# Values with the probabilities held fixed in the first eleven heads, and a branch sum in four column groups

## The chip, the core and the metric

The kernel runs on one core of a Trainium2 chip. The metric is device time in microseconds. The kernel before takes 192.63 us, the median of 8 runs (192.5 to 192.9). The core has five engines with queues of their own: PE (matrix multiply), DVE (vector), ACT (activation functions), POOL and SP; here SP issues nearly all transfers. [...]

## What is computed

Two branches on the same two rows `x` (batch 2, one position, 448 wide), and the residual:

```python
xn = layernorm(x)
# A: attention of one new position, 16 heads on 8 key/value heads, W = 4096 last positions
q = xn @ wq                                    # 448 -> 16 heads x 256
scores = q . k[last 4096] * 256 ** -0.5
o = softmax(scores) . v[last 4096]
a = o.reshape(2, 4096) @ wo                    # 4096 -> 448
# B: dense with a mish activation
h = xn @ w1 + b1                               # 448 -> 1792
b = (h * tanh(softplus(h))) @ w2               # 1792 -> 448
out = x + a + b
```

The caches hold 2 MB of K and 2 MB of V for each of the 16 pairs of key/value head and batch row. With the weights that is 77.7 MB to read.

## The kernel before

**Heads.** The program calls a pair (key/value head, batch row) a head; there are `NK` = 16, numbered 0 to 15, and each serves `rep` = 2 query heads. Key/value head `kvh` has heads 2 kvh and 2 kvh + 1. A head's 4096 positions lie as `T` = 32 tiles of 128 positions over the partitions, and are worked on in two halves of 16 tiles.

**A head's stages.**
- `load_k`, `load_v` (L327, L335): SP issues one 2 MB transfer each, K into one of 4 buffers, V into one of 5. The last V is cut into a half and two quarters. `load_wo` (L343) brings the slice of `wo` for a key/value head, the last one in two parts.
- `turn` (L352): DVE transposes half of K in 32x32 blocks.
- `scores` (L362): PE, 8 matmuls of 512 columns with a spread-out copy of q (`qdiag`, built by POOL in `build_q`, L241) as stationary operand; then ACT takes the exponential of 128x512 scores and their row sums.
- `turn_p` (L387): DVE transposes the probabilities. After the second half it forms `sums` by two small operations with the selector `hsel`; a small fp32 matmul, `den`, adds over the partitions, and DVE takes the reciprocal `rec`.
- `values` (L407): for each of 32 tiles and 2 column sets PE loads 128x128 of V as weights and streams the 2 columns of probabilities past it, 64 pairs of load and matmul, into a PSUM buffer (`ps_o`, 2 of them). DVE then scales by `rec` into `oT`, in bf16.
- `mix` (L433), once for each key/value head: the branch sum. PE multiplies `oT` (two stationary columns, one for each batch row) with the slice of `wo`, 8 matmuls of 224 columns.

**The branch sum's place.** The two output rows are summed in PSUM over the whole kernel, in `psA[0]` and `psA[1]`, 2x224 each, one bank each. `x` itself goes in first (2 matmuls, L209), then branch B (`dense_out`, L309, 28 matmuls, in loop turn 1), then the eight `mix`. At the end DVE copies one half to `res`, ACT the other, and one store writes the two rows.

**Order.** Every engine runs its instructions in the order in which the program writes them (`issue_in_order`, L17). Loop turn i (L457) issues the loads of K of head i+2 and V of head i, then the turns and scores of head i, with the probabilities turned one half later, then `build_q`, then `values` of head i-2 (`KA` = 2), and after an odd head its `mix`. Two further turns, 16 and 17, hold only the values of the last heads:

```python
        if i >= KA:
            values(i - KA)
            kvh, b = heads[i - KA]
            if b == Bsz - 1:
                mix(kvh)
```

So on PE a head's 64 value pairs stand behind the scores of the head two later, and DVE's scaling stands behind the turns of that later head.

Of the kernel before, what the change touches and what calls it, by code (L numbers as in the profile page):

```python
# [9 lines left out]
ALU = mybir.AluOpType  # L10
AXIS = mybir.AxisListType
BF16 = mybir.dt.bfloat16
FP32 = mybir.dt.float32
PSUM = bass.MemoryType.PSUM
# [20 lines left out]
def kernel(  # L35
# [13 lines left out]
    nc = tc.nc  # L49
    P = 128  # L50
    Q = 32
    NQ = P // Q

    Bsz, Sq, D = A_x.shape
    _, Hkv, Sk, Dh = A_k_cache.shape
    HqDh = A_wq.shape[1]
    Hq = HqDh // Dh
    rep = Hq // Hkv
# [3 lines left out]
    T = W // P  # L62
    NH = 2
    TH = T // NH
# [6 lines left out]
    ND = Dh // P  # L71
    NB = Dh // (2 * Q)
    NE = 2
    assert Sq == 1 and D * NX == NS * P and NS % 2 == 1 and HF % P == 0 and Hq % NX == 0
    assert TH * Q <= 512 and NB * NE * Q == Dh and ND == 2
    scale = float(Dh) ** -0.5
# [3 lines left out]
    ident = lead.tile([P, P], BF16)  # L80
    hsel = lead.tile([P, Q], FP32)
# [4 lines left out]
    consts = ctx.enter_context(tc.tile_pool(name="consts", bufs=1))  # L86
    p_pool = ctx.enter_context(tc.tile_pool(name="pp", bufs=3))
    small = ctx.enter_context(tc.tile_pool(name="small", bufs=3))
    ps_sc = ctx.enter_context(tc.tile_pool(name="ps_sc", bufs=2, space=PSUM))
    ps_o = ctx.enter_context(tc.tile_pool(name="ps_o", bufs=2, space=PSUM))  # L90
    ps_den = ctx.enter_context(tc.tile_pool(name="ps_den", bufs=1, space=PSUM))
    ps_a = ctx.enter_context(tc.tile_pool(name="ps_a", bufs=1, space=PSUM))
    ps_m = ctx.enter_context(tc.tile_pool(name="ps_m", bufs=1, space=PSUM))


    x_bf = consts.tile([Bsz, D], BF16)
# [14 lines left out]
    for lo, hi in ((0, SC), (SC, NS)):  # L111
        w = v_tile((hi - lo) * HW).rearrange("p (s n) -> p s n", n=HW)
# [2 lines left out]


    make_identity(nc, ident[:])
    eps_t = consts.tile([Bsz, 1], FP32)
    nc.vector.memset(eps_t[:], 1e-5)

# [7 lines left out]
        out=rstd[:], in_=mv[:, 1:2], func=ACT.Sqrt, bias=eps_t[:], scale=1.0  # L128
# [5 lines left out]
    for r in range(2):  # L134
        n = (NS + 1 - r) // 2
        nc.vector.tensor_scalar(  # L136
            out=xn_bf[:, r : NS : 2, :, :],
            in0=bass.AP(
                x_all.tensor,
                x_all.offset,  # L140
                [list(x_all.ap[0]), [1, n], [NS, P // 2], [(NS + r) // 2, 2]],
            ),
# [7 lines left out]
    for b4 in range(NB):  # L150
        rows = slice(b4 * Q, (b4 + 1) * Q)
        for j in range(NQ):
            nc.vector.tensor_copy(
                out=spread[rows, b4, j * Q : (j + 1) * Q], in_=ident[rows, rows]
            )
    hsel = hsel[:, 0:rep]
    nc.vector.tensor_copy(out=hsel, in_=ident[:, 0:rep])
    for j in range(1, NQ):
        nc.vector.tensor_tensor(
            out=hsel, in0=hsel, in1=ident[:, j * Q : j * Q + rep], op=ALU.add  # L160
        )
    ones_f = consts.tile([P, P], FP32)
    nc.gpsimd.memset(ones_f[:], 1.0)
# [2 lines left out]
    for i in range(NW):  # L166
        t = consts.tile([P, NB * NE, P], BF16, name=f"qdiag{i}")
# [5 lines left out]
    for s in range(NS):  # L173
# [7 lines left out]
        out=odd[:],  # L181
# [16 lines left out]
    nc.vector.memset(ones[:], 1.0)  # L198


    NO = 2
    DO = D // NO
    psA = [ps_a.tile([Bsz, DO], FP32, name=f"psA{n}") for n in range(NO)]

    def add(n, lhsT, rhs, **flags):
        nc.tensor.matmul(psA[n][:, :], lhsT=lhsT, rhs=rhs, skip_group_check=True, **flags)  # L206

    for n in range(NO):
        add(n, ident[0:Bsz, 0:Bsz], x_bf[:, n * DO : (n + 1) * DO], start=True, stop=False)  # L209


    qrep = consts.tile([P, NB, HH, NE, NX, Bsz], BF16)
# [28 lines left out]
    def build_q(i):  # L241
        kvh, b = heads[i]
        x, h0 = divmod(kvh * rep, HH)
        t = qdiag[i % NW]
        tv = t[:].rearrange("p (n e) c -> p n e c", e=NE)
        for j in range(NQ):
            rows = slice(j * Q, (j + 1) * Q)
            for e in range(NE):
                nc.gpsimd.tensor_copy(  # L249
                    out=tv[rows, :, e, j * Q : j * Q + rep],  # L250
                    in_=qrep[rows, :, h0 : h0 + rep, e, x, b],
                )

# [55 lines left out]
    def dense_out():  # L309
        w2_sb = dense.pop("w2")  # L310
        for x in range(NX):
            for c in range(NF):
                for n in range(NO):
                    add(
                        n,
                        act_bf[:, c, x, :],
                        w2_sb[:, x, c, n * DO : (n + 1) * DO],
                        start=False,
                        stop=False,
                    )  # L320


    NSTEP = len(heads) * NH
# [1 line left out]
    state = {}  # L325
# [26 lines left out]
    def turn(s):  # L352
        kt = kt_pool.tile([P, TH * Dh], BF16, tag="kt", name="kt")
        i, half = divmod(s, NH)
        k = k_t[i] if half < NH - 1 else k_t.pop(i)
        nc.vector.transpose(  # L356
            out=kt[:].bitcast(FP32),
            in_=k[:, half * TH * Dh : (half + 1) * TH * Dh].bitcast(FP32),
        )
        kt_t[s] = kt  # L360
# [26 lines left out]
    def turn_p(s):  # L387
        pT = p_pool.tile([P, TH * Q], BF16, tag="pT", name="pT", bufs=7)
        nc.vector.transpose(out=pT[:], in_=p_t.pop(s)[:])  # L389
        pT_t[s] = pT  # L390
        i, half = divmod(s, NH)
        if half != NH - 1:
            return
        rs = state.pop(("rs", i))
        sums = small.tile([P, rep], FP32, tag="sums", name="sums")
        nc.vector.tensor_scalar(
            out=sums[:], in0=hsel, scalar1=rs[:, 0:1], scalar2=None, op0=ALU.mult
        )
        nc.vector.scalar_tensor_tensor(  # L399
            out=sums[:], in0=hsel, scalar=rs[:, 1:2], in1=sums[:], op0=ALU.mult, op1=ALU.add  # L400
        )
        den = ps_den.tile([P, rep], FP32, tag="den", name="den")
        nc.tensor.matmul(den[:], lhsT=ones_f[:], rhs=sums[:], start=True, stop=True)  # L403
        state["rec", i] = small.tile([P, rep], FP32, tag="rec", name="rec", bufs=4)
        nc.vector.reciprocal(out=state["rec", i][:], in_=den[:])  # L405

    def values(i):  # L407
        kvh, b = heads[i]
        po = ps_o.tile([P, ND, rep], FP32, tag="o", name="o")
        vv = v_t.pop(i).rearrange("p t (m c) -> p t c m", c=ND)  # L410
        for t in range(T):
            half, th = divmod(t, TH)
            pTv = pT_t[i * NH + half][:].rearrange("p (t c) -> p t c", t=TH)
            for c in range(ND):
                nc.tensor.matmul(  # L415
                    po[:, c, :],
                    lhsT=vv[:, t, c, :],
                    rhs=pTv[:, th, 0:rep],
                    start=(t == 0 and c == 0),
                    stop=(t == T - 1),  # L420
                    skip_group_check=True,
                )
        if b == 0:
            state["oT"] = small.tile([P, ND, rep, Bsz], BF16, tag="oT", name="oT")
        oT = state["oT"]
        nc.vector.tensor_tensor(  # L426
            out=oT[:, :, :, b],
            in0=po[:],
            in1=state.pop(("rec", i))[:].unsqueeze(1).to_broadcast([P, ND, rep]),
            op=ALU.mult,  # L430
        )

    def mix(kvh):  # L433
        oT = state["oT"]
        w = wo_t.pop(kvh)
        for h in range(rep):
            for n in range(NO):
                for c in range(ND):
                    add(
                        n,  # L440
                        oT[:, c, h, :],
                        w[:, h, c * D + n * DO : c * D + (n + 1) * DO],
                        start=False,
                        stop=(kvh == Hkv - 1 and h == rep - 1 and c == ND - 1),
                    )

    NK = len(heads)
    KA = 2
# [5 lines left out]
    build_q(0)  # L454
    build_q(1)
    turn(0)
    for i in range(NK + KA):  # L457
        if i + 2 < NK:
            load_k(i + 2)
        if i < NK:  # L460
            load_v(i, (0, T) if i < NK - 1 else (0, T // 2, 3 * T // 4, T))
            kvh, b = heads[i]
            if b == Bsz - 1:
                load_wo(kvh, parts=1 if i < NK - 1 else 2)
            for half in range(NH):
                s = i * NH + half
                if s + 1 < NSTEP:
                    turn(s + 1)
                scores(s)
                if s >= 1:  # L470
                    turn_p(s - 1)
            if i + 2 < NK:
                build_q(i + 2)
        if i == NK:
            turn_p(NSTEP - 1)
        if i == 0:
            dense_in()
        if i == 1:
            dense_out()
        if i >= KA:  # L480
            values(i - KA)
            kvh, b = heads[i - KA]
            if b == Bsz - 1:
                mix(kvh)

    res = consts.tile([Bsz, D], BF16)
    nc.vector.tensor_copy(out=res[:, 0:DO], in_=psA[0][:, :])
    nc.scalar.copy(out=res[:, DO:D], in_=psA[1][:, :])  # L488
    nc.sync.dma_start(out=out.flatten_outer_dims(), in_=res[:])
    issue_in_order(tc)  # L490

# [29 lines left out]
```

The softmax here doesn't subtract the row's maximum and nothing guards it: scores larger than these inputs give would overflow.

## Time and profile before

| what | value |
|---|---|
| median of 8 runs | 192.63 us |
| the profiled execution | 192.62 us |
| its span (first to last instruction) | 190.7 us |
| mean granted clock of PE | 0.797 |
| busy: PE, its weight loads, DVE, ACT, POOL | 72%, 41%, 57%, 13%, 13% |
| PE loads and matmuls | 1592 each |
| data read | 77.67 MB, 407 GB/s over the span |

"Busy" is the time in which an engine runs at least one instruction, as a share of the span. A row of the page's groups reads: source line, engine, operation, output<-input, shape, count | busy time, mean duration in ns | idle time just before, and what ended it. The chain of work that ended last is followed back from the last instruction, each step to what released it. The row of slices cuts the span in 40 parts of 4.8 us and gives the busy share in tenths; for `PEclk` the clock that the throttle granted, 9 being 90% or more of full speed. Instruction counts of the built programs, and the arrival marks of a transfer's sixteen shares, are named as such.

### The profile page before, as it was taken

Reading aid. Unit: us, or ns where it says so; the run is one execution under the profiler, and the core shown is the slowest. Engines: PE = TensorE matmul, PEld = TensorE weight load, DVE = VectorE, ACT = ScalarE, POOL = GpSimd, SP = SyncE. Lnnn points to the kernel's source line nnn. Section 1 sums busy time; section 2 is a strip of 40 time slices with the busy share of each in tenths; the row PEclk is TensorE's granted clock in tenths of the full one; section 3 lists DMA queues with packets and bytes.
Section 4 is the critical chain, followed back from the end, with each engine's and each line's share of the span. In section 5 each row is a group of like instructions: output and inputs, shape, how many; then the busy total and the mean of one; then the engine's idle time right before and its main releaser. Section 6 shows DMA issues by size and latency. Waiting matters only on the chain.

```text
span 190.7 us, 3752 instructions
## 1 busy us (share of the span) xinstructions
PE 136.8 (72%) x1592; PEld 77.5 (41%) x1592; DVE 108.0 (57%) x169; ACT 25.4 (13%) x69; POOL 25.0 (13%) x139
## 2 busy tenths in 40 slices
PE   0242994699876959596759688696959493894984
PEld 0151373246552614344244435361535233362672
DVE  4706406895959390939366573939093754839301
ACT  5000110111210211011111111021102011021100
POOL 8005220010220201102020202020111100000000
PEclk9999995569996975888586957696678889589955
DMA  6999999999999999999999999999999999999970
GB/s 213 423 440 419 428 438 426 426 428 434 429 431 419 433 419 426 433 436 415 444 426 423 426 436 417 436 436 416 433 429 426 421 431 433 436 419 430 404 288 8
DMA packets 7818, 77.90 MB, mean 408 GB/s; under 512 B 757, under 2 KB 2809, under 8 KB 3322
## 3 DMA queue, kind: packets, MB, share of 16 engines
q1 hardware_dynamic: 7796, 77.66, 96.3%
q8 instruction: 12, 0.20, 0.4%
q14 instruction: 4, 0.03, 0.0%
q10 hardware_dynamic: 6, 0.01, 0.0%
HBM read 77.67 MB, written 0.00 MB: 407 GB/s over the span
## 4 chain that ended last, share of the span: by engine, by line
DMA 81%; DVE 8%; PE 8%; SPq 1%; issue 0%; ACT 0%
DMA k<-in_A_k_cache_dram 67%; DMA v<-in_A_v_cache_dram 13%; DVE kt L356 6%; PE sc L368 4%; PE psA L206 2%; DVE pT L389 1%; PE o L415 1%; SPq L113 0%; PE den L403 0%; SPq L260 0%; SPq L265 0%; SPq L330 0%; DVE oT L426 0%; DVE den_sb L305 0%; ACT res L488 0%
## 5 line engine op out<-in xcount | busy, mean ns | idle before, releaser
L356 DVE STREAM_TRANSPOSE kt<-k 128x2048 f32<-128x2048 f32 x32 | 73.5, 2299 | 44.4 <-DMA k<-in_A_k_cache_dram 44.4
L368 PE MATMUL sc<-kt,qdiag 128*128 128x512 bf16 x256 | 83.6, 484 | 15.7 <-DVE kt L356 12.2
L368 PEld LDWEIGHTS <-qdiag 128*128 128x128 bf16 x256 | 28.7, 121 | 56.4 <-issue 39.9
L378 ACT ACTIVATE p<-sc 128x512 bf16<-128x512 f32 x32 | 19.1, 598 | 144.8 <-PE sc L368 140.9
L249 POOL COPY qdiag<-qrep 32x8 bf16<-32x8 bf16 x128 | 21.0, 186 | 123.1 <-PE sc L368 108.3
L415 PEld LDWEIGHTS <-v 128*128 128x128 bf16 x1024 | 28.5, 98 | 5.7 <-issue 2.2
L415 PE MATMUL o<-pT,v 128*128 128x2 bf16 x1024 | 28.5, 163 | 0.9 <-DMA v<-in_A_v_cache_dram 0.8
L206 PE MATMUL psA<-wo,oT 128*2 128x224 bf16 x64 | 12.5, 370 | 14.5 <-DVE oT L426 14.5
L389 DVE STREAM_TRANSPOSE pT<-p 128x512 bf16<-128x512 bf16 x32 | 21.5, 671 | 0.0
L206 PEld LDWEIGHTS <-oT 128*2 128x2 bf16 x64 | 6.5, 111 | 17.8 <-DVE oT L426 15.2
L403 PEld LDWEIGHTS den<-sums,ones_f 128*128 128x128 f32 x32 | 6.5, 233 | 17.0 <-DVE sums L399 15.7
L403 PE MATMUL den<-sums,ones_f 128*128 128x2 f32 x32 | 6.5, 272 | 9.3 <-DVE sums L399 9.3
L405 DVE RECIPROCAL rec<-den 128x2 f32<-128x2 f32 x16 | 2.7, 170 | 16.0 <-PE den L403 16.0
L220 PE MATMUL qT_ps<-xs,v 128*128 128x4 bf16 x112 | 3.3, 166 | 5.5 <-DMA v<-in_A_wq_dram 3.0
L426 DVE TENSOR_TENSOR oT<-o,rec 128x4 bf16<-128x4 f32 x16 | 2.2, 136 | 7.4 <-PE o L415 7.4
L378 ACT ACTIVATION_READ_ACCUMULATOR p<-sc 128x1 f32 x32 | 6.2, 194 | 0.0
L220 PEld LDWEIGHTS <-v 128*128 128x128 bf16 x112 | 3.2, 104 | 6.0 <-DMA v<-in_A_wq_dram 6.0
L174 PE MATMUL xnT_ps<-ident,xn_bf 2*128 2x2 bf16 x7 | 0.5, 166 | 5.2 <-DVE xn_bf L136 5.2
L229 DVE CAST qT<-qT_ps 128x64 bf16<-128x64 f32 x1 | 0.2, 225 | 6.4 <-PE qT_ps L220 6.4
L399 DVE SCALAR_TENSOR_TENSOR sums<-hsel,rs,sums 128x2 f32<-128x2 f32 x16 | 3.5, 221 | 0.6
L275 PE MATMUL hT_ps<-xs,v 128*128 128x4 bf16 x49 | 3.7, 195 | 0.0
L275 PEld LDWEIGHTS <-v 128*128 128x128 bf16 x49 | 3.2, 151 | 0.3
(43 smaller groups left out, 28.3 us busy)
## 6 DMA issues: line engine op xcount, KB each, us to landing
k<-in_A_k_cache_dram SPq DMA_DIRECT2D x16, 2048.0 KB, 32.0
v<-in_A_v_cache_dram SPq DMA_DIRECT2D x15, 2048.0 KB, 35.0
v<-in_B_w_dram SPq DMA_DIRECT2D x2, 1568.0 KB, 21.0
wo<-in_A_wo_dram SPq DMA_DIRECT2D x7, 448.0 KB, 32.0
v<-in_A_wq_dram SPq DMA_DIRECT2D x1, 2048.0 KB
v<-in_A_wq_dram SPq DMA_DIRECT2D x1, 1536.0 KB, 10.7
v<-in_A_v_cache_dram SPq DMA_DIRECT2D x1, 1024.0 KB, 29.1
v<-in_A_v_cache_dram SPq DMA_DIRECT2D x2, 512.0 KB, 27.5
```

Of the source, the lines that this page charges most:

```text
L206: nc.tensor.matmul(psA[n][:, :], lhsT=lhsT, rhs=rhs, skip_group_check=True, **flags)
L220: nc.tensor.matmul(qT_ps[:, hh, e, :], lhsT=wq_v[s][:, hh, e, :], rhs=xs[:, s, :, :].rearrange("p x b -> p (x b)"), start=(s == 0), stop=( ...
L249: nc.gpsimd.tensor_copy(out=tv[rows, :, e, j * Q : j * Q + rep], in_=qrep[rows, :, h0 : h0 + rep, e, x, b],)
L275: nc.tensor.matmul(hT_ps[:, c, :, :].rearrange("p x b -> p (x b)"), lhsT=w1_v[:, s, c, :], rhs=xs[:, s, :, :].rearrange("p x b -> p (x b)" ...
L356: nc.vector.transpose(out=kt[:].bitcast(FP32), in_=k[:, half * TH * Dh : (half + 1) * TH * Dh].bitcast(FP32),)
L368: nc.tensor.matmul(psc[:], lhsT=qdiag[i % NW][:, n * NE + e, :], rhs=ktv[:, n, e, :, :], start=(n == 0 and e == 0), stop=(n == NB - 1 and ...
L378: nc.scalar.activation(out=p_sb[:], in_=psc[:].rearrange("p t c -> p (t c)"), func=ACT.Exp, scale=scale, accum_out=state["rs", i][:, s % N ...
L389: nc.vector.transpose(out=pT[:], in_=p_t.pop(s)[:])
L399: nc.vector.scalar_tensor_tensor(out=sums[:], in0=hsel, scalar=rs[:, 1:2], in1=sums[:], op0=ALU.mult, op1=ALU.add)
L403: nc.tensor.matmul(den[:], lhsT=ones_f[:], rhs=sums[:], start=True, stop=True)
L405: nc.vector.reciprocal(out=state["rec", i][:], in_=den[:])
L415: nc.tensor.matmul(po[:, c, :], lhsT=vv[:, t, c, :], rhs=pTv[:, th, 0:rep], start=(t == 0 and c == 0), stop=(t == T - 1), skip_group_check ...
```

## The change

Five things change:

1. **Values of heads 0 to 10** (`NFIX` = 5 heads stay as they were). The probabilities become the stationary operand: 4 columns, which are 2 tiles x 2 query heads. V streams past them, 2 tiles x 256 = 512 columns a matmul, 16 matmuls a head. Only the blocks in which a tile meets its own probabilities are used. ACT copies the 4x512 result to SBUF (`o_sb`).
2. **`finish`**, one head later, after the next head's first scores: four fp32 transposes on PE bring that result to 128 partitions in a PSUM buffer `q`; DVE copies one block and adds the other, then scales as before (`scale_o`).
3. **Heads 11 to 15** keep the 64 pairs (`values_fixed`), with the one buffer `q` as target. `mix` moves along: `close(i)` runs in the next loop turn for heads up to 13, for heads 14 and 15 right after their values. `mix(6)` thereby comes behind the last `den`.
4. **The branch sum** has four parts of 112 columns instead of two of 224. Each sits at its own PE column group (`tile_position=(0, 32 n)`) and its own 32 PSUM partitions, two parts to a bank. Each call of `add` issues four pairs. Four copies, two on DVE and two on ACT, bring the parts to the two rows of `res`; one store.
5. **Small parts.** The two query heads' columns lie 16 apart (`HS`) instead of side by side, in `hsel`, `build_q` and the probabilities. `den` shares a PSUM bank with earlier tiles (`ps_m`). DVE makes an fp32 identity at the start.

```diff
-    for n in range(NO):
-        add(n, ident[0:Bsz, 0:Bsz], x_bf[:, n * DO : (n + 1) * DO], start=True, stop=False)
+    NO = NQ
+    DO = D // NO
+    psA = [ps_a.tile([P, DO], FP32, name=f"psA{u}") for u in range(2)]
+
+    def part(n):
+        return psA[n // 2][n * Q : n * Q + Bsz, :]
+
+    def add(lhsT, w, start=False, stop=False):
+        for n in range(NO):
+            nc.tensor.matmul(
+                part(n),
+                lhsT=lhsT,
+                rhs=w[:, n * DO : (n + 1) * DO],
+                start=start,
+                stop=stop,
+                tile_position=(0, n * Q),
+                skip_group_check=True,
+            )
+
+    add(ident[0:Bsz, 0:Bsz], x_bf[:, :], start=True)
...
-                    out=tv[rows, :, e, j * Q : j * Q + rep],
+                    out=tv[rows, :, e, j * Q : (j + 1) * Q : HS],
...
     def values(i):
+        po = ps_o.tile([NR, NP * Dh], FP32, tag="o", name="o")
+        v = v_t.pop(i)
+        for u in range(T // NP):
+            half, uh = divmod(u, TH // NP)
+            nc.tensor.matmul(
+                po[:],
+                lhsT=pT_t[i * NH + half][:, uh * NP * Q : (uh + 1) * NP * Q : HS],
+                rhs=v[:, u * NP : (u + 1) * NP, :].rearrange("p t d -> p (t d)"),
+                start=(u == 0),
+                stop=(u == T // NP - 1),
+            )
+        o_sb = small.tile([NR, NP * Dh], FP32, tag="o_sb", name="o_sb", bufs=1)
+        nc.scalar.copy(out=o_sb[:], in_=po[:])
+        state["o", i] = o_sb
...
+    def finish(i):
+        ov = state.pop(("o", i))[:].rearrange("r (u m c) -> r u c m", u=NP, c=ND)
+        pq = ps_q.tile([P, NP * ND * NR], FP32, tag="q", name="q")
+        pqv = pq[:].rearrange("p (u c r) -> p u c r", u=NP, c=ND)
+        for u in range(NP):
+            for c in range(ND):
+                nc.tensor.transpose(pqv[:, u, c, :], ov[:, u, c, :], ident_f[0:NR, 0:NR])
+        o = small.tile([P, ND, rep], FP32, tag="osum", name="osum")
+        nc.vector.tensor_copy(out=o[:], in_=pqv[:, 0, :, 0:rep])
+        for u in range(1, NP):
+            nc.vector.tensor_tensor(
+                out=o[:], in0=o[:], in1=pqv[:, u, :, u * rep : (u + 1) * rep], op=ALU.add
+            )
+        scale_o(i, o[:])
...
+    NFIX = 5
+
+    def close(i):
+        if i < NK - NFIX:
+            finish(i)
+        kvh, b = heads[i]
+        if b == Bsz - 1:
+            mix(kvh)
+
     for i in range(NK + KA):
...
+                if half == 0 and i > KA:
+                    close(i - KA - 1)
...
         if i == NK:
             turn_p(NSTEP - 1)
+            close(i - KA - 1)
...
         if i >= KA:
-            values(i - KA)
-            kvh, b = heads[i - KA]
-            if b == Bsz - 1:
-                mix(kvh)
+            if i - KA < NK - NFIX:
+                values(i - KA)
+            else:
+                values_fixed(i - KA)
+        if i >= NK:
+            close(i - KA)
 
     res = consts.tile([Bsz, D], BF16)
-    nc.vector.tensor_copy(out=res[:, 0:DO], in_=psA[0][:, :])
-    nc.scalar.copy(out=res[:, DO:D], in_=psA[1][:, :])
+    for n in range(NO):
+        copy = nc.vector.tensor_copy if n // 2 == 0 else nc.scalar.copy
+        copy(out=res[:, n * DO : (n + 1) * DO], in_=part(n))
     nc.sync.dma_start(out=out.flatten_outer_dims(), in_=res[:])
```

More of the change, by code (lines that the diff above doesn't have):

```diff
@@ L73 @@
     NE = 2
+    HS = Q // rep
     assert Sq == 1 and D * NX == NS * P and NS % 2 == 1 and HF % P == 0 and Hq % NX == 0
@@ L90 @@
     ps_o = ctx.enter_context(tc.tile_pool(name="ps_o", bufs=2, space=PSUM))
-    ps_den = ctx.enter_context(tc.tile_pool(name="ps_den", bufs=1, space=PSUM))
+    ps_q = ctx.enter_context(tc.tile_pool(name="ps_q", bufs=1, space=PSUM))
     ps_a = ctx.enter_context(tc.tile_pool(name="ps_a", bufs=1, space=PSUM))
@@ L117 @@
     make_identity(nc, ident[:])
+    ident_f = consts.tile([Q, Q], FP32)
+    nc.vector.tensor_copy(out=ident_f[:], in_=ident[0:Q, 0:Q])
     eps_t = consts.tile([Bsz, 1], FP32)
@@ L156 @@
     hsel = hsel[:, 0:rep]
-    nc.vector.tensor_copy(out=hsel, in_=ident[:, 0:rep])
+    nc.vector.tensor_copy(out=hsel, in_=ident[:, 0:Q:HS])
     for j in range(1, NQ):
         nc.vector.tensor_tensor(
-            out=hsel, in0=hsel, in1=ident[:, j * Q : j * Q + rep], op=ALU.add
+            out=hsel, in0=hsel, in1=ident[:, j * Q : (j + 1) * Q : HS], op=ALU.add
         )
@@ L198 @@
     nc.vector.memset(ones[:], 1.0)
-    NO = 2
+    NO = NQ
     DO = D // NO
-    psA = [ps_a.tile([Bsz, DO], FP32, name=f"psA{n}") for n in range(NO)]
-    def add(n, lhsT, rhs, **flags):
-        nc.tensor.matmul(psA[n][:, :], lhsT=lhsT, rhs=rhs, skip_group_check=True, **flags)
-    for n in range(NO):
-        add(n, ident[0:Bsz, 0:Bsz], x_bf[:, n * DO : (n + 1) * DO], start=True, stop=False)
+    psA = [ps_a.tile([P, DO], FP32, name=f"psA{u}") for u in range(2)]
[13 more added lines that the diff above has]
+    add(ident[0:Bsz, 0:Bsz], x_bf[:, :], start=True)
     qrep = consts.tile([P, NB, HH, NE, NX, Bsz], BF16)
@@ L312, in dense_out @@
             for c in range(NF):
[L313 to L320, printed above, removed]
+                add(act_bf[:, c, x, :], w2_sb[:, x, c, :])
     NSTEP = len(heads) * NH
@@ L401, in turn_p @@
         )
-        den = ps_den.tile([P, rep], FP32, tag="den", name="den")
+        den = ps_m.tile([P, rep], FP32, tag="m", name="den")
         nc.tensor.matmul(den[:], lhsT=ones_f[:], rhs=sums[:], start=True, stop=True)
@@ L405, in turn_p, with scale_o, values_fixed @@
         nc.vector.reciprocal(out=state["rec", i][:], in_=den[:])
+    NP = 2
+    NR = NP * rep
     def values(i):
-        kvh, b = heads[i]
-        po = ps_o.tile([P, ND, rep], FP32, tag="o", name="o")
+        po = ps_o.tile([NR, NP * Dh], FP32, tag="o", name="o")
[12 more added lines that the diff above has]
+        state["o", i] = o_sb
+    def scale_o(i, o):
+        kvh, b = heads[i]
+        if b == 0:
+            state["oT"] = small.tile([P, ND, rep, Bsz], BF16, tag="oT", name="oT")
+        nc.vector.tensor_tensor(
+            out=state["oT"][:, :, :, b],
+            in0=o,
+            in1=state.pop(("rec", i))[:].unsqueeze(1).to_broadcast([P, ND, rep]),
+            op=ALU.mult,
+        )
[9 more added lines that the diff above has]
+        for u in range(1, NP):
+            nc.vector.tensor_tensor(
+                out=o[:], in0=o[:], in1=pqv[:, u, :, u * rep : (u + 1) * rep], op=ALU.add
+            )
+        scale_o(i, o[:])
+    def values_fixed(i):
+        pq = ps_q.tile([P, NP * ND * NR], FP32, tag="q", name="q")
+        po = pq[:, 0 : ND * rep].rearrange("p (c h) -> p c h", c=ND)
         vv = v_t.pop(i).rearrange("p t (m c) -> p t c m", c=ND)
@@ L417, in values @@
                     lhsT=vv[:, t, c, :],
-                    rhs=pTv[:, th, 0:rep],
+                    rhs=pTv[:, th, 0:Q:HS],
                     start=(t == 0 and c == 0),
@@ L422, in values @@
                 )
[L423 to L431, printed above, removed]
+        scale_o(i, po)
     def mix(kvh):
@@ L436, in mix @@
         for h in range(rep):
[L437 to L445, printed above, removed]
+            for c in range(ND):
+                add(
+                    oT[:, c, h, :],
+                    w[:, h, c * D : (c + 1) * D],
+                    stop=(kvh == Hkv - 1 and h == rep - 1 and c == ND - 1),
+                )
     NK = len(heads)
```

## The prediction

> **What bounds the kernel now.** I read the slices of the span first, then the chain that ended last, then the DMA queues, then TensorE's last 13 us.
>
> ```profile
> PEclk9999995569996975888586957696678889589955
> DMA  6999999999999999999999999999999999999970
> ```
>
> One digit is 4.8 us. The 16 DMA engines are full from the second slice to the 38th: 77.7 MB at some 428 GB/s set the time, and PE (72% busy) and DVE (57%) follow. What can move the end is the bytes, their split over the engines, and the few us after the last byte. The end of the chain (start, duration, work):
>
> ```profile
> 159.90 25.70 DMA v<-in_A_v_cache_dram
> 185.60 0.05 issue
> 185.65 0.60 PE o L415 x16
> 186.25 0.02 issue
> 186.28 0.17 DVE oT L426
> 186.45 0.04 issue
> 186.50 1.67 PE psA L206 x8
> 188.16 0.02 issue
> 188.19 0.34 ACT res L488
> ```
>
> The last quarter of the last V lands at 185.60; then 16 matmuls, a scale, the last branch sum's 8 matmuls and a copy. The store is issued at 188.55, and 2.2 us of closing work follow that nothing touches. The profiled execution took 192.62 us, its span 190.7, so 1.9 lie around it; the median is 192.63, so a difference in the span goes straight to the median.
>
> The queues hold what is less plain:
>
> ```profile
> q1 hardware_dynamic: 7796, 77.66, 96.3%
> q8 instruction: 12, 0.20, 0.4%
> ```
>
> q8 brings PE's instructions: 12 packets of 16 KB from 17.4 to 184.9 us, about one whenever PE has passed another 256. A packet holds one of the 16 engines for 0.88 to 0.96 us. The trace marks the arrival of each sixteenth of a transfer. For V's last quarter the marks form three groups: eight at 182.37 to 183.40, five at 183.99 to 184.35, three at 185.36 to 185.61. Eleven fetches had run, and 5x1 + 3x2 = 11. For a transfer that landed at 138.3, after eight fetches, there are eight early and eight late marks; after the ninth a single mark stands at 153.97, the one before it at 152.85. So **each fetch sets one engine back some 1.07 us for good**, the first eight hit eight engines, and a landing waits for the engine with most fetches, at the end one with two.
>
> **Fetches removed.** Early heads have 16 load/matmul pairs instead of 64 (11x48 = 528 fewer) and 4 transposes each (44 more); the branch sums go from 2+28+64 to 4+56+128 pairs (94 more). That is 390 pairs, 780 instructions. The built programs hold 3204 and 2432 on PE: 12.5 blocks of 256 become 9.5, so 9 fetches. If the first eight again fall on eight engines, the last V lands with one fetch on the worst: 185.60 - 1.07 = 184.53, and the last K, which paces the tail, at 168.9 instead of 169.9. [...]
>
> **Values of heads 0 to 10.** 64 pairs took 1.74 us a head. The new 16 matmuls stream 512 columns like
>
> ```profile
> L368 PE MATMUL sc<-kt,qdiag 128*128 128x512 bf16 x256 | 83.6, 484 | 15.7 <-DVE kt L356 12.2
> ...
> L378 ACT ACTIVATE p<-sc 128x512 bf16<-128x512 f32 x32 | 19.1, 598 | 144.8 <-PE sc L368 140.9
> ```
>
> which start 0.43 us apart at half clock (94.9 to 95.7) and about 0.22 at full (8 in 1.90 us): 3.5 to 6.9 us a head, so +1.7 to +5.1. A pair of heads has 20.5 us of DMA and PE is now busy 16 of them at a mean clock of 0.75. With 32 such matmuls a head, PE needs 6.9/c us at clock c, and some 1.5 for sums, denominators and transposes, out of 10.3: enough from c = 0.78 on. The clock rose to full after busy stretches (41.8, after scores without a gap) and fell after idle ones, so a PE that lags is a PE at full clock, at 8.4 us. I cost this at nothing. Its cover: V's buffer for head 9 is refilled by an issue at 96.98, and its old content was used up at 87.2 (values of head 4), 10 us earlier; and data land 32 us after their issue, so the queue stays full even when an issue is late. Heads 11 to 15 keep the short form and let PE catch up. Without that cover each us of lag is a us.
>
> ACT's copy of 4x512 stands near the 0.60 us row, 11 times, in ACT's 145 us of idling. **Added waits:** the transposes wait for that copy and are placed one head later, after the next head's first scores; it is long done. Behind them on PE wait a branch sum and scores. DVE's gather of 4x128 results (three ops, 0.2 + 0.2 + 0.14 us) waits for the transposes, 4 x 0.2 to 0.3 us by the denominator's row (272 ns, fp32); behind it is DVE's transpose of the next K, which waits for DMA 44 us in all. In return DVE no longer waits for an early head's values. The first dense sum (2.84 us) gets twice the pairs, 1.5 to 2.9 us, between transfers. The extra DVE copy (0.1) and the strided selection of columns on DVE and POOL change no sizes; POOL idles 123 us, and no DMA waits for either. The DMA queue's order has the same 47 entries; nothing is moved past it.
>
> **The tail up to the last V.** Two things get later on PE. Branch sum 6 (0.93 us at 180.11) filled a gap before the last denominator (181.09); it now comes after it, in front of head 14's values. And heads 14 and 15 share one PSUM buffer, so head 15 waits for head 14's scaling, 0.4 us instead of running on (x96 in one run before). Shifted by the earlier K: denominator 180.0, sum until 180.75 to 181.05, head 14 (26 ns a pair) until 182.85, head 15's first half from 183.0 to 183.9, third quarter to 184.4. The last quarter lands at 184.53, so this is just hidden, by 0.1 to 0.4 us. If the cover is gone it costs up to 0.5.
>
> **The last branch sum.** 8 matmuls of 224 columns started 0.187 us apart (half clock), 1.65 us. Now 16 of 112 in four column groups. Side by side, a pair can start every 27 ns, as the values' pairs do; in turn, every 93 ns (half of 187), 1.4 us plus the drain as before. [...] I take 30 ns; 93 is the other end.
>
> **Copies.** ACT: 0.598 us for 512 elements and 0.335 for 224 make 0.23 for 112, twice 0.47; DVE (0.38 for 224) twice 0.27, starting a little earlier. So 0.50 instead of 0.34: +0.15.
>
> **The sum.** V at 184.53; its 16 matmuls, scale and waits take 0.90 as before: 185.43. First half of the sum 0.24. The second half's weights landed at 186.80 (last mark) before, unused until 187.2; 1.07 earlier they land at 185.73. So the second half starts at 185.78 and ends 7 x 0.03 + 0.29 later: 186.28 instead of 188.15. Copies to 186.82, store at 186.85: 1.7 earlier than 188.55. 192.63 - 1.7 = **190.9**.
>
> **Rivals.**
> 1. The ninth fetch hits the last weights. [...] The old twelfth (184.9) shows no late mark, so its engine was done. On an engine still busy it moves the weights to about 186.65: sum until 187.2, store 187.77, gain 0.8: 191.8.
> 2. Fetches again double up on an engine before V's end (fewer fetches, same split, or the marks have another cause): V at 185.60, sum from 186.50, weights 186.80, end 187.35, store 187.92: 192.0.
> 3. The column groups take turns: 185.43 + 15 x 0.093 + 0.29 = 187.1, store 187.7: 191.8; with sum 6 at half clock (1.5 us) head 15 runs 0.5 late: 192.3. I take 192.0. With rival 2 on top it is no gain.
> 4. Slower: PE falls behind in heads 0 to 10 because the clock doesn't rise. At c = 0.6 a head takes 11.5 + 1.5 = 13.0, 2.7 behind each, 30 over eleven; the last five heads give back 2.3 each (8.0 of 10.3 busy), so the end is 18 late: 211. It decides from c = 0.70, where the lag of 11 us is just given back. For it: the clock row shows 5 or 6 in 14 of 40 slices. Against: those slices follow waits for K.
>
> **Chances.** Forecast 0.36; rival 1 0.22; rival 2 0.14; rival 3 0.17; rival 4 and other losses 0.08; smaller gains 0.03. About 0.2% (0.4 us) is what a measurement of this kernel tells from no change. Faster takes the first three, two thirds of rival 3: 0.83; the rest of rival 3 and the small gains: 0.09; slower 0.08. The range goes from 190.6 (a tail without the wait for weights) to 192.3, the late end of rival 3, and leaves out rival 4.
>
> **What would show it.** Right: 9 fetches on q8; V's last quarter near 184.5 with two groups of marks; the last sum's 16 matmuls within 0.9 us, their starts some 30 ns apart; DMA slices as full as before; the store near 186.9. Wrong: V's last quarter still at 185.6; starts 93 ns apart; a gap in the DMA row after 50 us, or PE at half clock while K waits in its buffers.

## The result

The changed kernel takes 191.04 us (median of 11 runs, 190.45 to 192.0) against 192.63 (31 runs, 192.43 to 193.05): ratio 0.9922, 95% interval 0.9910 to 0.9933. The forecast was 190.9, range 190.6 to 192.3. The spread has grown from 0.6 to 1.6 us, which the forecast did not say; it turns out to matter for the account of the forecast.

### The profile page after: what moved, and what is told of

It reads as the page before. It is cut to its first block, busy times and chain, and to the rows that moved or that the text cites. A ratio compares the mean times of both kernels' runs of the same rounds, so it can differ in the third digit from the quotient of the medians.

```text
span 189.5 us, 3026 instructions
## 1 busy us (share of the span) xinstructions
PE 145.8 (77%) x1202; PEld 71.2 (38%) x1202; DVE 114.8 (61%) x193; ACT 31.9 (17%) x81; POOL 27.2 (14%) x139
## 4 chain that ended last, share of the span: by engine, by line
DMA 84%; DVE 7%; PE 5%; SPq 1%; issue 0%; ACTq 0%; ACT 0%
DMA k<-in_A_k_cache_dram 37%; DMA v<-in_A_v_cache_dram 19%; DMA wo<-in_A_wo_dram 17%; DMA v<-in_B_w_dram 12%; DVE kt L364 5%; PE q L470 3%; PE sc L376 2%; DVE pT L397 2%; PE psA L214 1%; SPq L114 0%; PE den L411 0%; DVE sums L407 0%; DVE oT L439 0%; SPq L275 0%; SPq L338 0%
## 5 line engine op out<-in xcount | busy, mean ns | idle before, releaser
L376 PE MATMUL sc<-kt,qdiag 128*128 128x512 bf16 x256 | 73.8, 438 | 11.4 <-DVE kt L364 11.4
L376 PEld LDWEIGHTS <-qdiag 128*128 128x128 bf16 x256 | 25.1, 107 | 49.8 <-issue 28.6
L424 PE MATMUL o<-v,pT 128*4 128x512 bf16 x176 | 40.8, 386 | 0.0
L424 PEld LDWEIGHTS <-pT 128*4 128x4 bf16 x176 | 14.6, 88 | 25.7 <-issue 6.6
L432 ACT COPY o_sb<-o 4x512 f32<-4x512 f32 x11 | 6.3, 575 | 33.3 <-PE o L424 33.3
L470 PEld LDWEIGHTS <-v 128*128 128x128 bf16 x320 | 9.0, 100 | 1.6 <-issue 1.1
L470 PE MATMUL q<-pT,v 128*128 128x2 bf16 x320 | 9.1, 165 | 0.3 <-DVE oT L439 0.3
L452 PE MATMUL q<-ident_f,o_sb 4*128 4x4 f32 x44 | 7.0, 261 | 0.0
L214 PE MATMUL psA<-wo,oT 128*2 128x112 bf16 x128 | 4.0, 268 | 3.5 <-DVE oT L439 3.5
L452 PEld LDWEIGHTS q<-ident_f,o_sb 4*128 4x128 f32 x44 | 6.0, 206 | 0.2
L235 PEld LDWEIGHTS <-v 128*128 128x128 bf16 x112 | 3.1, 104 | 5.0 <-issue 3.0
```

The lines of the kernel that those rows point to most:

```text
L214: nc.tensor.matmul(part(n), lhsT=lhsT, rhs=w[:, n * DO : (n + 1) * DO], start=start, stop=stop, tile_position=(0, n * Q), skip_group_check ...
L235: nc.tensor.matmul(qT_ps[:, hh, e, :], lhsT=wq_v[s][:, hh, e, :], rhs=xs[:, s, :, :].rearrange("p x b -> p (x b)"), start=(s == 0), stop=( ...
L376: nc.tensor.matmul(psc[:], lhsT=qdiag[i % NW][:, n * NE + e, :], rhs=ktv[:, n, e, :, :], start=(n == 0 and e == 0), stop=(n == NB - 1 and ...
L424: nc.tensor.matmul(po[:], lhsT=pT_t[i * NH + half][:, uh * NP * Q : (uh + 1) * NP * Q : HS], rhs=v[:, u * NP : (u + 1) * NP, :].rearrange( ...
L432: nc.scalar.copy(out=o_sb[:], in_=po[:])
L452: nc.tensor.transpose(pqv[:, u, c, :], ov[:, u, c, :], ident_f[0:NR, 0:NR])
```

## The profile after

The profiled execution took 191.38 us, its span 189.5: a run from the slower half. Slices of its span, in the form shown for before:

```profile
PEclk9999995769999699988999699966999999669675
DMA  6999999999999999999999999999999999999990
```

The transfers are as dense as before, and the clock row falls less often to 5 or 6 although PE has more to do. One stage of the early heads, before and after, from the table of windows (window, its length, then busy us and instructions of PE, its loads, DVE, ACT and POOL, granted clock, DMA share, GB/s):

```profile
100.00:120.00 20.00, 16.21 (x172) 8.48 (x172) 11.74 (x15) 2.75 (x8) 2.65 (x16) 0.75 1.01 427
100.00:120.00 20.00, 17.21 (x90) 7.38 (x88) 12.65 (x20) 3.64 (x10) 2.94 (x16) 0.91 1.01 428
```

PE's busy time rose by 1 us in 20, and its clock from 0.75 to 0.91. A matmul stands in the traces as two instructions, the load of its stationary operand (its weights) and the matmul that streams the moving one: 1592 of each before, 1202 after. The new values cost 3.62 us a head at full clock (16 matmuls from 95.40 in this trace) instead of 1.74; at the higher clock the scores, which did not change, took 73.8 us in all instead of 83.6. The queues:

```profile
q1 hardware_dynamic: 7796, 77.66, 96.9%
q8 instruction: 9, 0.15, 0.3%
```

Nine instruction packets instead of twelve. The end of the chain (start, duration, work):

```profile
175.36 3.01 PE sc L376 x8
178.37 1.67 PE q L470 x64
...
181.66 0.30 PE psA L214 x16
181.96 1.79 PE q L470 x64
183.75 0.02 issue
183.77 0.18 DVE oT L439
183.95 0.04 issue
183.99 1.86 PE q L470 x64
185.85 0.02 issue
185.87 0.18 DVE oT L439
186.05 0.04 issue
186.09 0.65 PE psA L214 x16
186.74 0.23 ACT res L547
```

Before, this chain ended in the landing of V's last quarter. Here no transfer stands in it from 168.8 on: V's last quarter landed at 184.46, head 15's 64 pairs ran from 183.99 to 185.83 without a pause, and PE was the late one. So in this profile most of the earlier landing brings nothing: the last sum starts only 0.41 us earlier than before (186.09 for 186.50). The second half of head 15's scores (the first line) took 3.0 us because the clock had fallen to half at 175.7. The store is issued at 187.30, 1.25 us earlier than before.

The arrival marks tell of the landing. The table sorts the sixteen marks of V's last quarter into early (up to 183.6), late (183.7 to 184.7) and very late ones, for one profiled execution of each kernel of this study; the median is that of all its runs (a fetch that starts within about 1 us of the landing may not count yet, as before's twelfth, at 184.91, 0.69 us ahead of it: eleven fetches account for 5 late and 3 very late marks; whether an 8 KB packet of the queue q14, 0.31 us each in before and the change, put a mark over a border was not shown):

| kernel | fetches begun before the landing | early / late / very late | last mark of V | last mark of the last weights | median us |
|---|---|---|---|---|---|
| before | 12 | 8 / 5 / 3 | 185.60 | 186.80 | 192.63 |
| the change | 8 | 7 / 9 / 0 | 184.46 | 185.63 | 191.04 |
| sum alone | 13 | 8 / 4 / 4 | 185.65 | 186.78 | 191.87 |
| values alone | 8 | 8 / 8 / 0 | 184.15 | 185.46 | 192.10 |
| change + filler | 12 | 7 / 6 / 3 | 185.81 | 186.87 | 192.11 |
| before, 16 tiles | 9 | 8 / 7 / 1 | 185.64 | 186.72 | 192.51 |
| before, 8 tiles | 8 | 9 / 7 / 0 | 184.23 | 185.37 | 191.46 |
| tail order | 8 | 7 / 9 / 0 | 184.27 | 185.39 | 191.11 |
| tail order, 3 fixed | 8 | 8 / 8 / 0 | 184.26 | 185.39 | 190.59 |
| clock kept | 8 | 7 / 9 / 0 | 184.46 | 186.92 | 191.96 |
| the change again | 8 | 7 / 9 / 0 | 184.60 | 187.00 | 191.72 |
| tail order, 3 fixed, clock kept | 7 | 8 / 8 / 0 | 184.38 | 185.51 | 192.31 |

## The experiments

The theory: the transfers set the time, each instruction fetch puts one DMA engine back 1.07 us, and the change gains by fewer fetches ahead of the last V and by a shorter last sum. The rival: the fetches don't matter, and the gain is the tail's alone.

**The column groups alone.** All heads keep the 64 pairs, in the order and with the one PSUM buffer that the change gives to the late heads.

```diff
-    NFIX = 5
+    NFIX = 16
```

> The branch sum in four column groups alone: all 16 heads keep the 64 pairs (with the single PSUM buffer of the late heads). PE's program has 3399 instructions, so 13 fetches, 12 of them before the last V. Theory (each fetch sets one DMA engine back 1.07 us): V's last quarter lands at 185.6 as before or a little later, three groups of arrival marks; only the tail gains: last sum 0.54 us instead of 1.65, copies 0.15 longer: 191.8 to 192.1. Rival (the fetches don't matter, the gain came from the column groups and a steadier PE): as fast as the full change, 191.0.

191.87 us (191.7 to 192.94), ratio 0.9972 (0.9958 to 0.9987). As the theory has it: thirteen fetches, V at 185.65, and PE waits for it. Rows of its timeline (start, duration, engine, line, work, idle before it and what ended that):

```profile
183.69 1.45 PE L470 MATMUL q<-pT,v 128*128 128x2 bf16 x48 [0.25 <-DVE oT L439]
185.69 0.59 PE L470 MATMUL q<-pT,v 128*128 128x2 bf16 x16 [0.55 <-DMA v<-in_A_v_cache_dram]
186.54 0.65 PE L214 MATMUL psA<-wo,oT 128*2 128x112 bf16 x16 [0.26 <-DVE oT L439]
```

The sum starts where it did before (186.54 for 186.50) and takes 0.65 us instead of 1.65: the tail's share of the gain, 0.8 us with the four copies.

**The new values alone.**

```diff
-    NO = NQ
+    NO = 2
...
-        return psA[n // 2][n * Q : n * Q + Bsz, :]
+        return psA[n][0:Bsz, :]
...
-                tile_position=(0, n * Q),
...
```

> The new values of heads 0 to 10 alone: the branch sum stays in two parts of 224 columns with two copies. 2244 instructions on PE, so 8 fetches. Theory: V's last quarter at 184.4 to 184.5, two groups of marks; the last sum takes 1.65 us again, so 0.9 to 1.0 slower than the full change: 191.9 to 192.1. Rival (fetches don't matter): V at 185.6 and no faster than before, 192.6 or more.

192.10 us (191.23 to 192.97), ratio 0.9970 (0.9948 to 0.9991). V lands at 184.15 with two groups of marks, but the time gains less than the landing. In its profiled run (192.11) branch sum 6, now ahead of head 14's values, ran at half clock for 1.65 us, head 15 ran through without waiting for V, and the last sum began at 186.07 and took 1.65. In that run PE's own chain had used up the earlier landing.

**As many instructions as before.** After each early head's 16 matmuls:

```diff
-    psA = [ps_a.tile([P, DO], FP32, name=f"psA{u}") for u in range(2)]
+    psA = [ps_a.tile([P, DO + 2], FP32, name=f"psA{u}") for u in range(2)]
...
+        for _ in range(35):
+            nc.tensor.matmul(
+                psA[0][0:2, DO : DO + 2],
+                lhsT=ident[:, 0:2],
+                rhs=ident[:, 0:2],
...
+            )
```

> The full change plus 35 pairs of a 128x2 load and a 2-column matmul after each early head's values, into PSUM columns that nothing reads: 3202 instructions on PE, as many as before, 12 fetches. They cost PE about 1 us a head, beside the transfers. Theory: V's last quarter lands at 185.4 to 185.6 again, with a third group of marks, the last sum starts at 186.4 to 186.6, and the time is 191.8 to 192.1. Rival (the earlier landing has another cause, such as PE's reads of V or the column groups): V stays at 184.5 and the time at 191.0.

192.11 us (191.78 to 192.98), ratio 0.9977 (0.9959 to 0.9995). Twelve fetches, and the third group of marks is back: V at 185.81, K of head 15 at 169.69 instead of 168.78. In its profiled run head 15's values did not wait for V either; the sum began at 186.99. The late K moved PE's chain, and the second scores of head 15 took 3.13 us at half clock (from 176.6). So the time is the expected one, but in that run not by a wait for V. What the run does show is that the landing follows the instruction count, with the new values and the column groups in place.

**Fewer instructions, nothing else of the change.** In the kernel before:

```diff
-        for t in range(T):
+        n = T if i >= 11 else T // 2
+        for t in range(n):
...
-                    stop=(t == T - 1),
+                    stop=(t == n - 1),
```

> The kernel before, with the values of heads 0 to 10 over only 16 of their 32 tiles, which leaves out half of those heads' sum over positions: 2500 instructions on PE, 9 fetches, all other work and all transfers the same. Theory: V's last quarter at 184.5 with two groups of marks and everything behind it 1.07 us earlier: 191.5 to 191.6. Rival (fetches don't matter): 192.6, since PE's work there is hidden.

192.51 us (191.61 to 192.7), ratio 0.9984 (0.9971 to 0.9997): 0.1 us instead of 1.1, so on the time alone the theory had failed. The marks say why. K of head 15 came at 168.47 instead of 169.93, and V's third quarter at 182.94 instead of 184.37. But the ninth fetch began at 183.16, before V had landed: fifteen marks stand by 184.18 and a single one at 185.64. That this fetch met an engine with a share of V still to come is read from the marks; the traces do not name a packet's engine.

```profile
182.99 0.59 PE L416 MATMUL o<-pT,v 128*128 128x2 bf16 x16 [0.22 <-DMA v<-in_A_v_cache_dram]
185.68 0.59 PE L416 MATMUL o<-pT,v 128*128 128x2 bf16 x16 [2.11 <-DMA v<-in_A_v_cache_dram]
```

PE sat idle 2.11 us for that one share. The next run takes this fetch away, with `T // 4` in the place of `T // 2`:

> The kernel before, with the values of heads 0 to 10 over only 8 of their 32 tiles, which leaves out three quarters of those heads' sum over positions: 2148 instructions on PE, 8 fetches. In the run with 16 tiles the ninth fetch, at 183.2, set a single share of V's last quarter back to 185.64. Theory (that one fetch took the whole gain): no ninth fetch, so V's last quarter at 184.2 to 184.5, the store 1.1 to 1.4 us earlier than before, 191.3 to 191.6. Rival (the fetches are not what counts): 192.5 as with 16 tiles.

191.46 us (191.22 to 191.6), ratio 0.9933 (0.9918 to 0.9948). V lands at 184.23 with no very late mark, and the sum begins at 185.35 instead of 186.50:

```profile
181.55 3.55 PE L416 MATMUL o<-pT,v 128*128 128x2 bf16 x128
185.35 1.65 PE L206 MATMUL psA<-wo,oT 128*2 128x224 bf16 x8 [0.26 <-DVE oT L427]
```

The kernels with 16 and with 8 tiles differ in work that is hidden beside the transfers, and in one block of instructions more or less. The old kernel gains 1.2 us by fewer PE instructions alone. Here PE also reads less of V, but the run with the filler, in which all of V is read, puts that rival aside: with it the landing is late again.

**The tail's order.** In the changed kernel, two PSUM buffers for heads 11 to 15, and sum 6 ahead of the last denominator:

```diff
-        pq = ps_q.tile([P, NP * ND * NR], FP32, tag="q", name="q")
+        pq = ps_o.tile([P, NP * Dh], FP32, tag="o", name="o")
...
             turn_p(NSTEP - 1)
-            close(i - KA - 1)
...
-        if i >= NK:
+        if i >= NK - 1:
             close(i - KA)
```

> The full change, but heads 11 to 15 use the two PSUM buffers that the early heads leave free, and branch sum 6 stands right behind head 13's values again, ahead of the last denominator. Same instructions but one, 9 fetches. Theory (in the changed kernel PE's own chain after the last K sets the end, not V): head 15 no longer waits 0.26 us for head 14's scaling, and 0.3 us of sum 6 leave the chain: 0.3 to 0.6 faster than the full change, 190.5 to 190.8. Rival (V's landing sets the end): 191.0.

191.11 us, ratio 0.9917 (0.9892 to 0.9942): inconclusive by its median, since its six times lie in two clumps, 190.45 to 190.62 and 191.60 to 191.79. The profiled run is the fastest. There PE again waits for V, and the sum begins at 185.16:

```profile
184.31 0.59 PE L470 MATMUL o<-pT,v 128*128 128x2 bf16 x16 [0.40 <-DMA v<-in_A_v_cache_dram]
```

Of the slow clump there is no profile. Its runs have a mean clock of 0.849 to 0.867, the fast ones 0.886 to 0.896, so PE's clock may have a part in it. The same with three heads in the short form instead of five (`NFIX = 3`), hence 2255 instructions:

> The same as the run with the new tail order, but only heads 13 to 15 keep the 64 pairs (3 instead of 5): 2255 instructions on PE, 8 fetches, so no fetch in the last microseconds. Theory: heads 11 and 12 cost PE more (3.6 instead of 1.8 us each), still beside the transfers; no late share of V or of the last weights: 190.3 to 190.6, and a narrower spread than the full change's 190.45 to 192.0 if the ninth fetch causes part of it. Rival (the spread comes from PE's clock alone): same spread, same time as the run with 5.

190.59 us (190.44 to 190.89), ratio 0.9891 (0.9876 to 0.9907), beyond the full change's interval: the fastest version here. No fetch begins after 183.2, and none of its four times lies in a slow clump. Its eighth fetch begins at 183.18, as early as the ninth of the run with 16 tiles, and leaves no very late mark: that fits an engine which had no fetch before.

```profile
181.37 3.52 PE L470 MATMUL o<-pT,v 128*128 128x2 bf16 x128
185.15 0.67 PE L214 MATMUL psA<-wo,oT 128*2 128x112 bf16 x16 [0.26 <-DVE oT L439]
186.45 0.34 SPq L547 DMA_DIRECT2D out_dram<-res  x1
```

**PE's clock in the tail.** The full change, with 8 idle matmuls after head 15's first scores:

```diff
+        kt = kt_t.pop(s)
...
+        if s == 2 * len(heads) - 2:
+            fill = ps_o.tile([NR, NP * Dh], FP32, tag="o", name="fill")
+            for u in range(8):
+                nc.tensor.matmul(
+                    fill[:], lhsT=ident[:, 0:NR], rhs=kt[:, 0:512], start=True, stop=True
+                )
```

> The full change plus 8 matmuls of 512 columns right after the first half of head 15's scores, into PSUM that nothing reads, where PE otherwise idles 1.8 us. Theory (in the profiled run of the change the clock fell to half at 175.7 for lack of work just ahead, and head 15's second scores took 3.0 instead of 1.9 us): the clock stays at full there, the last denominator comes at 180.0 instead of 181.3, the last sum starts at 185.3 to 185.6 instead of 186.1: 190.5 to 190.8. Rival (PE's clock in the tail costs nothing because V lands late enough): 191.0 or, with the filler in the way, more.

191.96 us (191.32 to 192.25), ratio 0.9957 (0.9939 to 0.9974), slower than expected, though PE did what was expected: second scores 1.91 us, last denominator at 179.93, sum from 185.35. The sum then broke in two:

```profile
185.35 0.35 PE L214 MATMUL psA<-wo,oT 128*2 128x112 bf16 x8 [0.26 <-DVE oT L446]
186.96 0.36 PE L214 MATMUL psA<-wo,oT 128*2 128x112 bf16 x8 [1.26 <-DMA wo<-in_A_wo_dram]
```

The second part of the last weights had fifteen marks by 185.59 and one at 186.92, with the ninth fetch begun at 184.93. That is the prediction's first rival, which had put the weights at 186.65. The full change once more, unaltered:

> The full change once more, unaltered, for another profile and more times on the same chip as the next run. Theory (its spread of 190.45 to 192.0 is the ninth fetch, which either meets an engine that still has a share of the last weights or one that is done): times in two clumps, near 190.6 and near 191.7, and a profile in which the last weights' sixteen marks end at 185.4 to 185.7 when the time is near the first, or a single late mark near 186.8 when it is near the second. Rival (the phase of PE's clock makes the spread): times spread evenly, and no single late mark in either.

Six times of 190.87 to 192.05, median 191.72, beside 192.57 for before: 0.85 us by the medians; the ratio, 0.9934 (0.9914 to 0.9954), would be some 1.3 us, so the size of this repetition's gain is less certain. The profiled run was the slowest, and it shows the same:

```profile
184.65 0.59 PE L470 MATMUL q<-pT,v 128*128 128x2 bf16 x16 [0.47 <-DMA v<-in_A_v_cache_dram]
185.49 0.35 PE L214 MATMUL psA<-wo,oT 128*2 128x112 bf16 x8 [0.26 <-DVE oT L439]
187.04 0.35 PE L214 MATMUL psA<-wo,oT 128*2 128x112 bf16 x8 [1.19 <-DMA wo<-in_A_wo_dram]
```

Here everything up to the sum runs as forecast, 185.49 for 185.43, and one late share of the weights (187.00) costs 1.19 us. So the same kernel has two kinds of profile: late weights (this one, 192.05 us), and none but a late PE (the first one, 191.38). The times are not cleanly in two clumps, as the fetch alone would have it; that the fetch and PE's clock together make the spread fits both profiles, but how much is due to each was not measured. When the ninth fetch begins does not decide it plainly either: at 184.73 and 184.90 (the change and the new tail order) the weights were on time, at 184.93 and 185.01 one share was late.

**All together.** New tail order, three short heads, and the idle matmuls:

> New tail order, three heads with the 64 pairs, and the 8 matmuls that keep the clock up: 2271 instructions on PE, 8 fetches. Theory (with the fetches gone V's landing at 184.3 sets the end again, and PE is already within 0.3 us of it): the same as without the filler, 190.4 to 190.7. Rival (PE's clock in the tail still costs): 0.3 or more faster than without it, 190.3 or less.

192.31 us (191.35 to 193.77), ratio 0.9993 (0.9970 to 1.0016): a clear miss of both, and the whole gain is gone. In the profiled run the clock was at half from 165.9 to 172.7, so head 12's values, 16 matmuls of 512 columns here, ran until 175.2 and had taken up PE's idle time. The idle matmuls then stood in the way, and the sum began at 188.49 although V was there at 184.38.

```profile
170.57 4.64 PE L431 MATMUL o<-v,pT 128*4 128x512 bf16 x16
175.15 1.91 PE L377 MATMUL sc<-kt,qdiag 128*128 128x512 bf16 x8
176.99 1.89 PE L387 MATMUL fill<-kt,ident 128*4 128x512 bf16 x8
```

Whether its slower median comes from the filler in every run is open. Its ninth fetch (188.6) came after the data.

## Why the prediction was right, step by step

- **Transfers set the time, early values are hidden:** right. PE's 3.62 us a head leave the DMA row full, V of head 9 is issued at 96.95 (96.98 before), and the clock rose from 0.75 to 0.91.
- **Fetches removed:** right, also in size. V's last quarter at 184.46 for 184.53, K of head 15 at 168.78 for 168.9, the last weights at 185.63 for 185.73. The runs with 16 and 8 tiles show the effect without the rest of the change. V's landing moved by 1.14 us, from 185.60 to 184.46. (The built programs differ by 772 instructions, not 780; that moves no fetch.)
- **Tail up to V, "just hidden, by 0.1 to 0.4 us":** this step failed in the first profile, and held in the repeated one. The sum assumed full clock, as before; with half a clock from 175.7 the last denominator came at 181.27 for 180.0, and the last sum at 186.09 for 185.43. The run with the idle matmuls bears this out: with the clock full until 179.6 the denominator came at 179.93 and the sum at 185.35. I had named the cover and priced its loss at up to 0.5 us; it cost 0.66.
- **Last branch sum:** side by side, as taken. Of its 16 matmuls four start within 10 ns, and the last two fours follow 93 ns apart, at half clock; 0.54 us in all for 1.65. Loads of the second four began 2 to 12 ns after the fourth matmul, in the same rows; in the kernel before, a load at 186.64 began 2 ns after the start of the matmul ahead of it, also in the same rows. The 30 ns between single matmuls were the wrong picture with the right sum.
- **Copies:** 0.56 us on DVE and 0.52 on ACT for an estimate of 0.50; from the sum's end (186.63) to the store 0.67 instead of 0.57.
- **Sum of the terms:** the forecast had 1.07 us from an earlier start of the last sum, 0.8 from a shorter sum, and 0.17 lost on the copies: 1.7. In the first profile the start gave 0.41, the sum 1.11 (it ran without a break, as the weights were there at 185.63), and the copies took 0.27: 1.25, store at 187.30 for 186.85. In the repeated profile the start gave 1.01, but with late weights the sum lasted 1.90 instead of 1.65, and with the copies 0.49 is left: store at 188.06, for rival 1's 187.77. So the forecast's terms did not all come out in either profile, and that the median fell within 0.15 us of 190.9 is in part luck: the first profile gains 1.25 us by other shares than the forecast's, the repetition had a median of 191.72, and the change's fast end, 190.45, which lies 0.15 below the forecast's range, has no profile.
- **Rivals:** rival 1 (late weights), at 0.22 beside the forecast's 0.36, is there in the repeated profile and not in the first. Rivals 2, 3 and 4 were not seen: V did not land at 185.6, the groups did not take turns, PE did not fall behind in heads 0 to 10.

## What to carry to other kernels

When the DMA engines are full all the time, look at how evenly they finish, not only at bytes: the sixteen arrival marks of the last transfer tell whether a few shares come late, and here they came late with PE's instruction fetches (three very late ones with twelve fetches, none with eight). A change that makes the last transfer land earlier is worth only what the engines behind it can follow (here 0.41 us of 1.14 in one profile), so price the tail at the slow clock too (head 15's second scores took 3.01 us, and 1.91 with the clock kept up), and allow for a wider spread where two late-comers are within a microsecond (here 1.6 us for 0.6; how much of it is due to either was not measured). A filler in an idle gap is safe only as long as the gap is there in every run: with it the last sum began at 185.35 in one kernel and at 188.49 in another.

## What the runs showed of the hardware

- One 16 KB instruction packet took 0.88 to 0.96 us. In the kernel before, the sixteen marks of the four transfers that landed after the ninth fetch (145.45), from 149.11 to 159.89, end in a single late one, 1.07 to 1.16 us behind the mark ahead of it; those of the four behind the tenth fetch (161.42), from 165.08 to 175.85, end in two, 1.01 to 1.08 us behind. No profile with eight fetches or fewer ahead of V's landing has a very late mark; with nine to thirteen there are one to four. So the first eight seem to fall on eight engines and later ones on engines that already had one; no trace names the engine. One ninth fetch, at 183.16, cost a whole landing 1.4 us (185.64 against 184.23 without it).
- In this case the program with more matmul columns ran PE at a higher clock (0.88 for 0.80 over the span), and spent little more busy time (146 us for 137).
- In the kernel before, each of the twelve rises of the clock from 41.8 us on came after 3.4 us in which PE was busy for 82% or more, and eleven of the twelve falls from 58.8 on after 3.4 us with 36 to 62%; in the changed kernel PE was busy 1.59 of the 3.41 us ahead of the fall at 175.7. But a busy PE alone did not hold the clock. In the kernel before PE was busy 3.1 of the 3.4 us from 178.3 to 181.7, most of it with 2-column matmuls, and the clock fell to half at 181.7. In the old kernel with 8 tiles PE was busy 9.7 of the 10.2 us from 176.1 to 186.3, again with 2-column matmuls for more than half of it, and the clock stayed at half (both branch sums in it took 1.65 us).
- Four matmuls in four column groups, all with the same 128 rows, started within 10 ns of each other.
